# Six value buffers, five probability buffers, attention loads moved ahead, and first products that wait for half of a weight unit

## The chip, the cores and the metric

The kernel runs on one core of a Trainium2 chip. The metric is the device time of one execution in microseconds (us). Five engines work side by side, each through its own instructions in their order: PE (TensorE, matrix products), DVE (VectorE), ACT (ScalarE), POOL (GpSimd) and SP (SyncE), which here only issues transfers. They wait for each other through semaphores.

## What is computed

```python
attn = softmax_masked(q @ k.T / 8) @ v            # q, k, v: (2, 8, 576, 64)
# heads 0..3: keys of the last 32 positions; heads 4..7: keys at the same position modulo 32
x = attn.transpose(0, 2, 1, 3).reshape(1152, 512)
h = np.maximum(x @ w_in, 0.0)                     # w_in (512, 2048)
x = h * h @ w_out                                 # w_out (2048, 512)
p = domain_probs / domain_probs.sum(-1)           # (1152, 4)
out = sum(p[:, e:e+1] * (np.maximum(x @ w1[e], 0.0) @ w2[e]) for e in range(4))
```

The weights of the first pair (w_in, w_out) come as 64-bit numbers; the kernel makes two 32-bit parts of each itself.

## The kernel before

Attention is cut into 16 groups: `Strided` (heads 4 to 7, 8 units of 54 or 36 queries) and `Local` (heads 0 to 3, 128 or 64 queries). One group (`attend`, L461) is: three loads (k, q, v), scores on PE (L363 to L367 or L430 to L438), maximum on DVE (L485), exponentials on ACT (L490, or L495 on DVE and L496 on ACT), sums and reciprocals on DVE (L497 to L499), normalizing on POOL (L500), transposes on PE (L372 or L442), a copy on ACT (L480), products with the values on PE (L384 or L452), and the result into x in two parts, on ACT (L509) and DVE (L513). Six groups are `startup`, seven `second`, three `third`.

The first pair of products runs over x in three blocks of 384 tokens (x_75, x_76, x_77 in the order's names) and over weight units in w buffers (w_80 to w_89). A unit is loaded and converted in two halves (L562): a 512 KB load (L568), ACT (L575), three DVE steps (L580, L584, L589), ACT (L595) and POOL (L599). A product of 128x384 stands as three matmuls, L617, L618 and L619, which the text calls a round. Four rounds into a bank bh make one step x @ w_in (L639); relu and square follow on ACT and DVE (L650, L654, L657, L660), and give h; four rounds into banks by are its h @ w_out (L681). The first eight steps use block x_75 alone, and need eight units, w_80 to w_87. Afterwards blocks 1 and 2 use the same units again. The experts (L834 to L836, and L617 to L619 again) follow, and are not touched by the change.

The order of everything is made when the program is built: `Plan.run` takes tasks with estimated lengths, rank, needs and buffer rings, and starts on each engine the ready task of lowest rank. The instructions are then written in the order of these starts. A change of a ring, a rank or an estimate thus reorders all engines. While PE has nothing before its first products, the plan puts in matmuls on a zero tile (`warm`, L961), called fillers below. Rings that matter here: q and k with 4 buffers, v with 4 (`NQ`), p (probabilities) with 3 (`NP`), and 2 banks ba for attention, beside banks by in the first six groups.

Of the kernel before, what the change touches and what calls it, by code (L numbers as in the profile page):

```python
# [16 lines left out]
P = 128  # L17
B, H, S, D = 2, 8, 576, 64
# [3 lines left out]
TB = 384  # L22
NB = NT // TB
KD = DM // P
CH = 256
# [136 lines left out]
def tile_attention_mlp_experts(ctx: ExitStack, tc: tile.TileContext, a, out):  # L162
# [20 lines left out]
    def many(pool, name, n, shape, dtype=F32):  # L183
        return [pool.tile(shape, dtype, name=f"{name}{i}") for i in range(n)]
# [7 lines left out]
    CONV0 = 7431  # L192
    CONV = 9000
    FETCH = 2019
    WITH2 = 1082
    PE_SLICE = 863
    BASE = 3959
# [10 lines left out]
    NMID = 2  # L208
    NHID = 4
    NST = 5  # L210
    NP = 3
    NQ = 4
    NPT = 2
    NW = 10
    NS = 2
# [20 lines left out]
    plan.ring("bank_y", many(banks, "by", 4, [P, 512]))  # L236
    plan.ring("q", many(at, "q", NQ, [P, U * N3]))
    plan.ring("k", many(at, "k", NQ, [P, U * N3]))
    plan.ring("v", many(at, "v", NQ, [P, 512]))
    probs = many(at, "p", NP, [P, 512])  # L240
    plan.ring("p", probs)
    plan.ring("pt", many(at, "pt", NPT, [P, 512]))
# [9 lines left out]
    def mm_r(n):  # L252
        return int(n / 2.4) + 3
# [4 lines left out]
    def act(n):  # L258
        return n + 40
# [5 lines left out]
        return int(n * 2.05) + 190  # L265

    def dma(nbytes):
        return int(nbytes / 357) + 60


    n1, n2 = FF // P, F2 // P
# [5 lines left out]
    def due(n):  # L277

        return START + STEP * n + WITH * min(n, half) + WITH2 * min(max(n - half, 0), half)

# [177 lines left out]
    x_ready = {}  # L458
    attention_done = []

    def attend(g, rank, rings):  # L461
        env = {}
        n = g.units * g.cols
        loads = []
        for what, nbytes in zip("kqv", g.bytes):
            loads.append(plan.add({"dma": dma(nbytes)}, lambda e, w=what: g.load(env, w), rank=rank - 5000, take=[(env, what, [what])]))

        def view(x, pitch=g.pitch):
            return x[:, : g.units * pitch].rearrange("p (u c) -> p u c", u=g.units)[:, :, : g.cols]
# [50 lines left out]

    startup = [Strided(0, j) for j in range(3)] + [Local(0, j) for j in range(3)]
    for k, g in enumerate(startup):
        attend(g, BASE + EACH * k, ["bank_a", "bank_y"])
    second = [Local(0, 3), Local(0, 4)] + [Strided(1, j) for j in range(3)] + [Local(1, 0), Local(1, 1)]
    for k, g in enumerate(second):
        attend(g, START - AHEAD + k * (due(half) - START - END2) // len(second), ["bank_a"])
    third = [Local(1, j) for j in (2, 3, 4)]
    for k, g in enumerate(third):
        attend(g, due(half) - AHEAD + k * (due(2 * half) - due(half) - END3) // len(third), ["bank_a"])

    def open_late(e):
        attn.close()
# [23 lines left out]
    for u in sorted(when, key=lambda x: when[x]):  # L556
        kind, e_, c = u
        w_env[u] = {}
        wide_ = kind in ("wi", "wo")
        soon = wide_ and first[u] <= LAG  # L560
        rank = when[u] - (CONV0 if soon else CONV)
        for j in range(2):  # L562
            env = {}
            cs = slice(j * 2 * CH, (j + 1) * 2 * CH)

            def load(e, env=env, kind=kind, e_=e_, k=2 * c + j, wide_=wide_):
                if wide_:
                    nc.sync.dma_start(out=env["raw"], in_=a[kind][k].bitcast(U32))  # L568
                else:
                    nc.sync.dma_start(out=f32(env["raw"][:, : 2 * CH]), in_=a[kind][e_, k])  # L570

            def small(e, env=env):
                top = f32(env["raw"].rearrange("p (f t) -> p f t", t=2)[:, :, 1])
                if e == "act":
                    nc.scalar.activation(out=env["mid"], in_=top, func=AF.Copy, scale=EXP_SHIFT)  # L575
                else:
                    nc.vector.tensor_scalar(out=env["mid"], in0=top, scalar1=EXP_SHIFT, scalar2=None, op0=ALU.mult)

            def shift(e, env=env):
                nc.vector.tensor_scalar(out=env["val"].bitcast(U32), in0=env["mid"].bitcast(U32), scalar1=3, scalar2=0x7FFFFFF8, op0=ALU.logical_shift_left, op1=ALU.bitwise_and)  # L580

            def sign(e, env=env):
                v = env["val"].bitcast(U32)
                nc.vector.scalar_tensor_tensor(out=v, in0=env["mid"].bitcast(U32), scalar=0x80000000, in1=v, op0=ALU.bitwise_and, op1=ALU.bitwise_or)  # L584

            def low(e, env=env):
                v = env["val"].bitcast(U32)
                bits = env["raw"].rearrange("p (f t) -> p f t", t=2)[:, :, 0]
                nc.vector.scalar_tensor_tensor(out=v, in0=bits, scalar=29, in1=v, op0=ALU.logical_shift_right, op1=ALU.bitwise_or)  # L589

            def value(env=env, wide_=wide_):
                return env["val"] if wide_ else f32(env["raw"][:, : 2 * CH])

            def hi(e, u=u, cs=cs, value=value):
                nc.scalar.activation(out=weights(u)[:, 0, cs], in_=value(), func=AF.Copy)  # L595

            def lo(e, u=u, cs=cs, value=value):
                w = weights(u)
                eng[e].tensor_tensor(out=w[:, 1, cs], in0=value(), in1=f32(w[:, 0, cs]), op=ALU.subtract)  # L599

            t = plan.add({"dma": dma(P * 4 * CH * 4 if wide_ else P * 2 * CH * 4)}, load, after=[chain["dma"]], rank=rank - FETCH, take=[(env, "raw", ["raw"])])
            chain["dma"] = t
            n = 2 * CH
            if wide_:
                t = plan.add({"act": act(n)}, small, after=[t], rank=rank, take=[(env, "mid", ["mid"])])
                t = plan.add({"dve": dve(n // 2)}, shift, after=[t], rank=rank + 500, take=[(env, "val", ["val"])])
                t = plan.add({"dve": dve(n)}, sign, after=[t], rank=rank + 700, free=[(env, "mid")])
                t = plan.add({"dve": dve(n)}, low, after=[t], rank=rank + 1200, free=[(env, "raw")])
            t = plan.add({"act": act(n)}, hi, after=[t, chain["w"]], rank=rank + 2000, take=[(w_env[u], "w", ["w"])] if j == 0 else [], quiet=not wide_)
            chain["w"] = t  # L610
            lo_engines = {"pool": pool(n)} if wide_ else {"dve": dve(n)}
            t = plan.add(lo_engines, lo, after=[t], rank=rank + R_LO, free=[(env, "val") if wide_ else (env, "raw")], quiet=not wide_)
            w_ready.setdefault(u, []).append(t)
# [19 lines left out]
    for n in range(moe1 + LAG):  # L633
        if n < moe1:
# [3 lines left out]
            for pos, kk in enumerate((2, 3, 0, 1)):  # L638
                def product(e, env=env, u=u, b=b, i=i, kk=kk, pos=pos):  # L639
                    w = w_in(u)  # L640
                    cs = slice((i % 2) * P, (i % 2 + 1) * P)
                    mm3(env["H"][:, :TB], w[:, 0, kk, cs], w[:, 1, kk, cs], xt[b][:, 0, kk], xt[b][:, 1, kk], pos == 0, pos == 3)

                freed = [(w_env[u], "w")] if pos == 3 and last_use[u] == n else []
                previous = plan.add({"pe": 3 * mm_r(TB)}, product, after=[previous if pos else None, *x_ready[b, (0, 1) if kk < 2 else (2, 3)], *w_ready[u]], rank=due(n) + pos * PE_SLICE, take=[(env, "H", ["bank_h"])] if pos == 0 else [], free=freed, adds=[("bank_y", [spare])] if n == 0 and pos == 0 else ())
            t = previous
            rank = due(n) - URGENT

# [402 lines left out]
```

## Time and profile before

| | |
|---|---|
| median of 3 runs | 647.59 us (647.18 to 648.01) |
| profiled execution | 647.54 us, of it span of the trace 645.8 us |
| PE busy | 631.5 us, 98% of the span |
| DVE busy | 360.8 us, 56% |
| ACT, POOL busy | 235.6 us, 105.9 us |

The span is measured from the first instruction to the last. "Busy" of PE counts modelled ends of overlapping matmuls, so that a share near 100% says that PE has no idle gap, and not that it is at its peak. A gap of an engine is shown in brackets with what ended it.

### The profile page before, as it was taken

What the parts mean: (1) busy time and instruction counts of PE and PEld (TensorE: products, weight loads), DVE (VectorE), ACT (ScalarE), POOL (GpSimd) and SP (SyncE); (2) the same over time, 40 slices, a digit from 0 to 9 for tenths busy, and PEclk for the clock granted to TensorE, in tenths of its full rate; (3) what the DMA queues carried; (4) which work ended last, traced back from release to release, by engine and by line L of the source; (5) the groups of instructions that cost most, each with busy time, mean ns of one, the idle gap of its engine ahead of it and who ended that gap; (6) DMA issues with size and microseconds to landing.
All of it is one profiled execution on the core that took longest, in us unless ns stands there. A gap on an engine that the chain in (4) does not pass through costs nothing.

```text
span 645.8 us, 9891 instructions
## 1 busy us (share of the span) xinstructions
PE 631.5 (98%) x3868; PEld 580.2 (90%) x3868; DVE 360.8 (56%) x664; ACT 235.6 (36%) x527; POOL 105.9 (16%) x119
## 2 busy tenths in 40 slices
PE   7998999999999999999999999999999999999997
PEld 4777889999999999999999999999999999999997
DVE  4898886288623264945557415557324557643512
ACT  2956675354423244522333312333212333321110
POOL 2435341033100000030112000113001012400000
PEclk9998999999999999999999999999999999999999
DMA  8976434034300023231133301123301222100201
GB/s 276 265 228 179 150 127 131 0 100 145 98 1 1 1 65 98 72 91 38 38 94 136 89 1 50 63 90 110 81 1 50 81 82 97 33 2 0 98 2 49
DMA packets 28990, 53.51 MB, mean 83 GB/s; under 512 B 4432, under 2 KB 10000, under 8 KB 28944
## 3 DMA queue, kind: packets, MB, share of 16 engines
q1 hardware_dynamic: 28944, 52.89, 26.7%
q8 instruction: 30, 0.49, 0.3%
q14 instruction: 16, 0.13, 0.1%
HBM read 50.52 MB, written 2.36 MB: 82 GB/s over the span
## 4 chain that ended last, share of the span: by engine, by line
PE 88%; DVE 5%; ACT 2%; DMA 2%; issue 1%; POOL 1%; SPq 1%; DVEq 0%; ACTq 0%; POOLq 0%
PE bh L617 14%; PE bh L618 14%; PE bh L619 14%; PE by L835 8%; PE by L836 8%; PE by L834 8%; PE by L617 5%; PE by L619 4%; PE by L618 4%; PE ba L836 2%; PE ba L835 2%; PE ba L834 2%; DVE val L580 1%; DVE val L589 1%; DVE val L584 1%
## 5 line engine op out<-in xcount | busy, mean ns | idle before, releaser
L617 PE MATMUL bh<-x,w 128*128 128x384 f32 x416 | 141.8, 341 | 1.7 <-DVE h L660 1.7
L619 PE MATMUL bh<-x,w 128*128 128x384 f32 x416 | 139.8, 336 | 0.0
L618 PE MATMUL bh<-x,w 128*128 128x384 f32 x416 | 139.7, 336 | 0.0
L872 DVE TENSOR_TENSOR c<-bh,c 128x384 f32<-128x384 f32 x80 | 43.1, 556 | 85.9 <-ACT c L885 58.4
L836 PE MATMUL by<-w,h 128*128 128x512 f32 (+1 forms) x232 | 89.0, 384 | 0.0
L835 PE MATMUL by<-w,h 128*128 128x512 f32 (+1 forms) x232 | 89.0, 384 | 0.0
L834 PE MATMUL by<-w,h 128*128 128x512 f32 (+1 forms) x232 | 88.5, 382 | 0.0
L617 PEld LDWEIGHTS bh<-x,w 128*128 128x128 f32 x416 | 78.5, 189 | 4.7 <-DVE h L660 3.2
L618 PEld LDWEIGHTS bh<-x,w 128*128 128x128 f32 x416 | 78.5, 189 | 1.0
L619 PEld LDWEIGHTS bh<-x,w 128*128 128x128 f32 x416 | 78.4, 188 | 0.0
L779 POOL TENSOR_TENSOR sf<-raw 128x256 f32<-128x256 f32 x16 | 12.1, 755 | 347.1 <-DMA raw<-in_w_dram 283.8
L617 PE MATMUL by<-h,w 128*128 128x384 f32 x192 | 65.5, 341 | 0.3 <-ACT h L657 0.3
L618 PE MATMUL by<-h,w 128*128 128x384 f32 x192 | 64.5, 336 | 0.6 <-DVE h L660 0.6
L619 PE MATMUL by<-h,w 128*128 128x384 f32 x192 | 64.6, 336 | 0.0
L599 POOL TENSOR_TENSOR w<-val,w 128x512 fp32r<-128x512 f32 x32 | 43.3, 1361 | 76.4 <-ACT w L595 73.9
L654 DVE SCALAR_TENSOR_TENSOR bh<-bh,r 128x384 f32<-128x384 f32 x48 | 27.0, 562 | 51.0 <-ACT r L650 51.0
L929 DVE SCALAR_TENSOR_TENSOR h<-bh,h 128x384 fp32r<-128x384 f32 x32 | 17.8, 557 | 64.0 <-ACT h L926 64.0
L904 ACT ACTIVATE h<-c 128x384 fp32r<-128x384 f32 x64 | 31.8, 518 | 54.6 <-DVE c L872 34.5
L836 PEld LDWEIGHTS by<-w,h 128*128 128x128 f32 x232 | 43.6, 188 | 8.5
L834 PEld LDWEIGHTS by<-w,h 128*128 128x128 f32 x232 | 43.6, 188 | 8.0
L835 PEld LDWEIGHTS by<-w,h 128*128 128x128 f32 x232 | 43.6, 188 | 8.1
L599 DVE TENSOR_TENSOR w<-raw,w 128x512 fp32r<-128x512 f32 x64 | 43.1, 696 | 9.3 <-ACT w L595 9.3
(122 smaller groups left out, 1039.2 us busy)
## 6 DMA issues: line engine op xcount, KB each, us to landing
raw<-in_w_dram SPq DMA_DIRECT2D x64, 256.0 KB, 2.7
raw<-in_wi_dram SPq DMA_DIRECT2D x16, 512.0 KB, 3.7
raw<-in_wo_dram SPq DMA_DIRECT2D x16, 512.0 KB, 3.6
raw<-in_w_dram SPq DMA_DIRECT2D x16, 512.0 KB, 3.6
out_dram<-acc SPq DMA_DIRECT2D x8, 256.0 KB, 2.1
v<-in_vs_dram SPq DMA_DIRECT2D x6, 256.0 KB, 4.4
v<-in_vl_dram SPq DMA_DIRECT2D x8, 192.0 KB, 3.8
k<-in_kl_dram SPq DMA_DIRECT2D x8, 160.0 KB, 4.5
```

What stands on the lines that cost most here:

```text
L599: eng[e].tensor_tensor(out=w[:, 1, cs], in0=value(), in1=f32(w[:, 0, cs]), op=ALU.subtract)
L617: nc.tensor.matmul(dst, lhsT=wh, rhs=xh, start=start, stop=False)
L618: nc.tensor.matmul(dst, lhsT=wh, rhs=xl, start=False, stop=False)
L619: nc.tensor.matmul(dst, lhsT=wl, rhs=xh, start=False, stop=stop)
L654: nc.vector.scalar_tensor_tensor(out=h, in0=h, scalar=0.0, in1=env["r"], op0=ALU.max, op1=ALU.mult)
L779: nc.gpsimd.tensor_tensor(out=got(env["sf"])[:, 0], in0=part(env, 1, 0), in1=part(env, 1, 1), op=ALU.add)
L834: nc.tensor.matmul(o, lhsT=h[:, 0, ts], rhs=w[:, 0], start=start, stop=False)
L835: nc.tensor.matmul(o, lhsT=h[:, 0, ts], rhs=w[:, 1], start=False, stop=False)
L836: nc.tensor.matmul(o, lhsT=h[:, 1, ts], rhs=w[:, 0], start=False, stop=stop)
L872: return lambda e: nc.vector.tensor_tensor(out=got(c[key]), in0=c[bank][:, :TB], in1=got(c[other]), op=ALU.add)
L904: nc.scalar.activation(out=env["hid"][:, 0], in_=got(c[key]), func=AF.Relu)
L929: nc.vector.scalar_tensor_tensor(out=env["hid"][:, 1], in0=env["H"][:, :TB], scalar=0.0, in1=f32(env["hid"][:, 0]), op0=ALU.max, op1=ALU.s ...
```

## The change

The value ring gets six buffers of its own (`NV`), the probability ring five. The loads of the six startup groups get a rank 9000 ahead of their scores, the later ones 3500, where all had 5000. The estimated length of a load grows (310 bytes per ns instead of 357). The halves of a w_in unit are taken in the order 1, 0, and a product waits for the half that it reads, where it waited for both; x rows 2 and 3, which it takes first, are in half 1. FIRST is 0 and changes nothing.

```diff
-    NP = 3
+    NP = 5
     NQ = 4
+    NV = 6
+    LEAD0, LEAD = 9000, 3500
...
-    plan.ring("v", many(at, "v", NQ, [P, 512]))
+    plan.ring("v", many(at, "v", NV, [P, 512]))
...
-        return int(nbytes / 357) + 60
+        return int(nbytes / 310) + 60
...
-            loads.append(plan.add({"dma": dma(nbytes)}, lambda e, w=what: g.load(env, w), rank=rank - 5000, take=[(env, what, [what])]))
+            loads.append(plan.add({"dma": dma(nbytes)}, lambda e, w=what: g.load(env, w), rank=rank - lead, take=[(env, what, [what])]))
...
-        for j in range(2):
+        for j in (1, 0) if kind == "wi" else (0, 1):
...
-            t = plan.add({"act": act(n)}, hi, after=[t, chain["w"]], rank=rank + 2000, take=[(w_env[u], "w", ["w"])] if j == 0 else [], quiet=not wide_)
+            t = plan.add({"act": act(n)}, hi, after=[t, chain["w"]], rank=rank + 2000, take=[(w_env[u], "w", ["w"])] if u not in w_ready else [], quiet=not wide_)
...
-  after=[previous if pos else None, *x_ready[b, (0, 1) if kk < 2 else (2, 3)], *w_ready[u]]
+  after=[previous if pos else None, *x_ready[b, (0, 1) if kk < 2 else (2, 3)], w_ready[u][kk < 2]]
```

In the changed kernel all lines behind the edits stand three lower (L620 is the old L617). Names below end in the buffer's number.

**SP, loads of the first groups.** k, q, v are attention loads, raw is half of a weight unit. Before:

```order
L424 DMA v_122<-in_vl_dram 96x512
L568 DMA raw_90<-in_wi_dram 128x1024
L420 DMA k_115<-in_kl_dram 128x2x160
L422 DMA q_111<-in_ql_dram 128x256
L420 DMA k_116<-in_kl_dram 128x2x160
L422 DMA q_112<-in_ql_dram 128x256
L420 DMA k_117<-in_kl_dram 128x2x160
L568 DMA raw_91<-in_wi_dram 128x1024
```

After:

```order
L427 DMA v_122<-in_vl_dram 96x512
L423 DMA k_115<-in_kl_dram 128x2x160
L425 DMA q_111<-in_ql_dram 128x256
L427 DMA v_123<-in_vl_dram 96x512
L423 DMA k_116<-in_kl_dram 128x2x160
L425 DMA q_112<-in_ql_dram 128x256
L427 DMA v_124<-in_vl_dram 96x512
L571 DMA raw_90<-in_wi_dram 128x1024
```

Six loads of groups 5 and 6, their values among them, now stand ahead of the first weights.

**PE, around the first product of the first pair (L617, later L620).** Before:

```order
L384 MATMUL ba_106<-pt_126,v_121 64x36 x16
L442 MATMUL ba_105<-ident,p_124 96x128 x4
L452 MATMUL by_108<-pt_127,v_122 64x64 x8
L617 MATMUL bh_103<-x_75,w_80 128x384
L618 MATMUL bh_103<-x_75,w_80 128x384
L619 MATMUL bh_103<-x_75,w_80 128x384
```

After:

```order
L445 MATMUL by_108<-ident,p_125 96x128 x4
L436 LDWEIGHTS cb
L436 MATMUL ba_105<-cb 128x192
L441 MATMUL ba_105<-k_118,q_114 64x96 x4
L366 LDWEIGHTS cb
L366 MATMUL ba_106<-cb 128x432
L370 MATMUL ba_106<-k_115,q_111 54x54 x16
L455 MATMUL by_107<-pt_131,v_122 64x64 x8
L455 MATMUL ba_105<-pt_130,v_123 64x64 x8
L620 MATMUL bh_103<-x_75,w_80 128x384
```

The first product now stands behind the scores of two more groups (nine in all; before, seven) and behind a fifth set of value products.

**PE, where blocks of attention meet the products with w_83 (h_99 is the third h).** Before:

```order
L438 MATMUL ba_106<-k_118,q_114 64x96 x8
L617 MATMUL by_109<-h_99,w_83 128x384
L618 MATMUL by_109<-h_99,w_83 128x384
L619 MATMUL by_109<-h_99,w_83 128x384
L617 MATMUL by_108<-h_99,w_83 128x384
```

After:

```order
L441 MATMUL ba_106<-k_118,q_114 64x96 x8
L375 MATMUL ba_105<-ident,p_125 128x128 x4
L436 LDWEIGHTS cb
L436 MATMUL ba_105<-cb 128x192
L441 MATMUL ba_105<-k_115,q_111 64x96 x4
L387 MATMUL ba_106<-pt_130,v_123 64x36 x16
L620 MATMUL by_110<-h_99,w_83 128x384
```

Transposes, scores and value products of three groups, which were spread between products, now follow each other in the two banks ba.

**DVE, at the same place.** Before:

```order
L589 SCALAR_TENSOR_TENSOR val_95<-raw_90,val_95 128x512
L584 SCALAR_TENSOR_TENSOR val_96<-mid_94,val_96 128x512
L499 RECIPROCAL st_132<-st_132 128x8
L589 SCALAR_TENSOR_TENSOR val_96<-raw_91,val_96 128x512
L495 TENSOR_TENSOR p_124<-ba_105,st_128 128x8x36
```

After:

```order
L592 SCALAR_TENSOR_TENSOR val_95<-raw_90,val_95 128x512
L501 TENSOR_SCALAR st_132<-st_132 128x8
L502 RECIPROCAL st_132<-st_132 128x8
L516 TENSOR_TENSOR x_76<-ba_105,x_76 128x2x6x12
L583 TENSOR_SCALAR val_96<-mid_94 128x512
L657 SCALAR_TENSOR_TENSOR bh_103<-bh_103,r_101 128x384
L587 SCALAR_TENSOR_TENSOR val_96<-mid_94,val_96 128x512
L516 TENSOR_TENSOR x_77<-ba_105,x_77 128x24x12
L657 SCALAR_TENSOR_TENSOR bh_104<-bh_104,r_102 128x384
L663 TENSOR_TENSOR h_99<-bh_103,h_99 128x384
L592 SCALAR_TENSOR_TENSOR val_96<-raw_91,val_96 128x512
L663 TENSOR_TENSOR h_100<-bh_104,h_100 128x384
```

The eighth half of a weight unit (val_96 from raw_91), which followed the seventh closely, now comes behind results of attention and behind two squares.

## Rows read from the trace of the kernel before

**Rows 1.** By stretch: us, busy PE, PEld, DVE, ACT, POOL, granted clock, DMA share, GB/s.

```profile
5.00:28.00 23.00, 18.74 (x326) 13.42 (x323) 15.77 (x47) 12.93 (x52) 7.77 (x8) 1.00 1.01 298
28.00:45.00 17.00, 15.75 (x215) 13.34 (x212) 16.68 (x34) 11.15 (x28) 7.41 (x7) 1.00 0.79 243
45.00:61.00 16.00, 13.38 (x143) 11.46 (x143) 14.61 (x31) 8.94 (x20) 6.81 (x6) 0.98 0.66 194
61.00:71.00 10.00, 10.00 (x81) 9.24 (x79) 8.26 (x18) 7.50 (x24) 4.87 (x5) 0.86 0.45 150
...
110.00:646.00 536.00, 531.87 (x2806) 496.85 (x2804) 272.38 (x475) 168.75 (x337) 63.94 (x76) 1.00 0.19 60
```

**Rows 2.** PE's waits from 5 to 110 us: total us, times, longest.

```profile
PE ba L438 <- DMA q<-in_ql_dram: 2.4, 2, 1.4
PE ba L433 <- DVE x L513: 1.9, 1, 1.9
PE bh L617 <- DVE h L660: 1.1, 2, 0.9
...
PE ba L372 <- POOL p L500: 0.7, 1, 0.7
...
PE ba L363 <- DVE x L513: 0.2, 1, 0.2
```

**Rows 3.** Timeline of ACT and PE, first weights: start, length, what, idle before.

```profile
14.17 0.66 ACT L575 ACTIVATE mid<-raw 128x512 f32<-128x512 f32 x1 [3.66 <-DMA raw<-in_wi_dram]
...
26.61 0.44 PE L617 MATMUL bh<-x,w 128*128 128x384 f32 x1
```

**Rows 4.** Loads: how often, KB each, median us from issue to landing.

```profile
v<-in_vl_dram SPq DMA_DIRECT2D x8, 192.0 KB, 3.8
k<-in_kl_dram SPq DMA_DIRECT2D x8, 160.0 KB, 4.5
q<-in_ql_dram SPq DMA_DIRECT2D x8, 128.0 KB, 4.5
```

**Rows 5.** Timeline of PE: scores and value products of strided groups.

```profile
36.84 1.01 PE L367 MATMUL ba<-k,q 64*54 64x54 f32 x32
...
47.10 1.14 PE L384 MATMUL ba<-pt,v 54*64 54x54 f32 x32
```

**Rows 6.** Timeline of DVE and POOL: conversion steps beside POOL and alone.

```profile
33.16 2.55 POOL L599 TENSOR_TENSOR w<-val,w 128x512 fp32r<-128x512 f32 x2 [1.28 <-ACT w L595]
...
34.49 1.50 DVE L580 TENSOR_SCALAR val<-mid 128x512 uint32<-128x512 uint32 x1
...
37.03 0.41 DVE L580 TENSOR_SCALAR val<-mid 128x512 uint32<-128x512 uint32 x1
...
56.08 0.67 DVE L584 SCALAR_TENSOR_TENSOR val<-mid,val 128x512 uint32<-128x512 uint32 x1
56.19 1.71 POOL L599 TENSOR_TENSOR w<-val,w 128x512 fp32r<-128x512 f32 x1 [4.08 <-ACT w L595]
...
56.90 1.55 DVE L589 SCALAR_TENSOR_TENSOR val<-raw,val 128x512 uint32<-128x512 uint32 x1
```

**Rows 7.** Groups from 0 to 110 us: count, busy us, mean ns, idle before.

```profile
L580 DVE TENSOR_SCALAR val<-mid 128x512 uint32<-128x512 uint32 x22 | 15.4, 699 | 4.9 <-ACT mid L575 4.3 <-POOL w L599 0.3
```

**Rows 8.** The chain that ended last: exponentials of one local group.

```profile
82.48 1.40 ACT p L490 x8
```

**Rows 9.** Timeline of PE: the longest wait, half clock, and full clock.

```profile
58.87 0.24 PE L433 MATMUL ba<-cb 128*128 128x192 bf16 x1 [1.93 <-DVE x L513]
...
61.14 0.53 PE L618 MATMUL by<-h,w 128*128 128x384 f32 x1
61.46 0.53 PE L619 MATMUL by<-h,w 128*128 128x384 f32 x1
...
83.34 0.33 PE L619 MATMUL bh<-x,w 128*128 128x384 f32 x1
83.51 0.33 PE L617 MATMUL bh<-x,w 128*128 128x384 f32 x1
```

More of the change, by code (lines that the diff above doesn't have):

```diff
@@ L194, in tile_attention_mlp_experts @@
     FETCH = 2019
+    FIRST = 0
     WITH2 = 1082
@@ L459, in tile_attention_mlp_experts, with attend @@
     attention_done = []
-    def attend(g, rank, rings):
+    def attend(g, rank, rings, lead):
         env = {}
@@ L522, in tile_attention_mlp_experts @@
     for k, g in enumerate(startup):
-        attend(g, BASE + EACH * k, ["bank_a", "bank_y"])
+        attend(g, BASE + EACH * k, ["bank_a", "bank_y"], LEAD0)
     second = [Local(0, 3), Local(0, 4)] + [Strided(1, j) for j in range(3)] + [Local(1, 0), Local(1, 1)]
     for k, g in enumerate(second):
-        attend(g, START - AHEAD + k * (due(half) - START - END2) // len(second), ["bank_a"])
+        attend(g, START - AHEAD + k * (due(half) - START - END2) // len(second), ["bank_a"], LEAD)
     third = [Local(1, j) for j in (2, 3, 4)]
     for k, g in enumerate(third):
-        attend(g, due(half) - AHEAD + k * (due(2 * half) - due(half) - END3) // len(third), ["bank_a"])
+        attend(g, due(half) - AHEAD + k * (due(2 * half) - due(half) - END3) // len(third), ["bank_a"], LEAD)
     def open_late(e):
@@ L599, in lo @@
                 eng[e].tensor_tensor(out=w[:, 1, cs], in0=value(), in1=f32(w[:, 0, cs]), op=ALU.subtract)
-            t = plan.add({"dma": dma(P * 4 * CH * 4 if wide_ else P * 2 * CH * 4)}, load, after=[chain["dma"]], rank=rank - FETCH, take=[(env, "raw", ["raw"])])
+            t = plan.add({"dma": dma(P * 4 * CH * 4 if wide_ else P * 2 * CH * 4)}, load, after=[chain["dma"]], rank=rank - FETCH - (FIRST if first.get(u) == 0 else 0), take=[(env, "raw", ["raw"])])
             chain["dma"] = t
@@ L644, in tile_attention_mlp_experts @@
                 freed = [(w_env[u], "w")] if pos == 3 and last_use[u] == n else []
-                previous = plan.add({"pe": 3 * mm_r(TB)}, product, after=[previous if pos else None, *x_ready[b, (0, 1) if kk < 2 else (2, 3)], *w_ready[u]], rank=due(n) + pos * PE_SLICE, take=[(env, "H", ["bank_h"])] if pos == 0 else [], free=freed, adds=[("bank_y", [spare])] if n == 0 and pos == 0 else ())
+                previous = plan.add({"pe": 3 * mm_r(TB)}, product, after=[previous if pos else None, *x_ready[b, (0, 1) if kk < 2 else (2, 3)], w_ready[u][kk < 2]], rank=due(n) + pos * PE_SLICE, take=[(env, "H", ["bank_h"])] if pos == 0 else [], free=freed, adds=[("bank_y", [spare])] if n == 0 and pos == 0 else ())
             t = previous
```

## The prediction

> **What bounds the kernel now.** I read first the busy time by stretch [rows 1]. The reader is to see that from 110 us on PE is busy 531.9 of 536.0 us, and what is missing there is the end of the program. So the time after 110 us is the sum of the products, which the change leaves alone, and the change can only gain or lose what PE loses before. Next the same table for the beginning. From 28 to 45 us DVE is busy 16.7 of 17.0 us, from 45 to 61 us 14.6 of 16.0. There PE is fed by DVE: no round starts before DVE has converted its weights or has finished its h. From 61 us on PE has no gap for 10 us, since block 1 of x is there by then and each converted unit is used twice. Before 28 us the transfers are the limit: DMA share 1.01, 298 GB/s. Then PE's waits [rows 2]: thirteen rows, 9.3 us in all when added up, the longest single one 1.9 us for DVE's x. Last the clock: it is 0.98 and 0.86 in the stretches 45 to 61 and 61 to 71 [rows 1], which is 0.02 x 16 + 0.14 x 10 = 1.7 us lost; matmuls there start 0.32 us apart, at 1.2 GHz, where they start 0.17 us apart at 2.4 [rows 9], and the fall came after the 1.93 us wait. So 9.3 + 1.7 = 11.0 us, and the few fillers that stand in further gaps before the first product, are all that any order could give back.
>
> I count in PE's work: how much further PE is in the new order at the same time. Since PE is never short of work later, that lead at 110 us is the gain. The profiled execution took 647.54 us, the median is 647.59; I add to the first.
>
> **The first weights, 5 to 28 us.** The new order puts six loads ahead of the first half of weights: 2 x (192 + 160 + 128) KB [rows 4] = 0.98 MB, at 298 GB/s 3.3 us. The half landed at 14.1 us [rows 3] and will land near 17.4. Behind it on ACT stand its own copy, the exponentials of a group (1.40 us, rows 8) and the copy of the second half, which lands some 4 us later (the next six loads with the second half are 1.2 MB). I lay the new order on these lengths and find the first half ready on POOL near 25.0 us, and the first product at 28.0, where it was at 26.6 [rows 3]. Waiting for one half instead of two saves one conversion here (DVE 0.41 + 0.67 + 0.67 us [rows 6], then ACT and POOL), and hides most of the 3.3 us. In exchange PE has done one more set of scores (1.0 us) and one more of value products with its transposes (at most the 1.1 us of a strided group) [rows 5], against 1 or 2 rounds of 0.52 us less. The lead at 28 us is 1.0 to 1.6; I take 1.5, since the fifth probability buffer lets ACT and POOL go through the first groups without a stop. The two added buffers cost two more clears on POOL at the very start, where POOL is idle until its first normalizing.
>
> **28 to 45 us.** By the order, DVE has as many conversions behind it when it makes the first h, and more of the attention; it starts that h without the 1.5 us step that met POOL [rows 6]. Walked through, the two first h are done at 37 and 38 us, some 2.4 us earlier, and PE, which waits 1.6 us for the first of them, has at 45 us three rounds and one set of transposes and values more behind it: lead 2.5.
>
> **45 to 61 us: what the change adds.** Here the new order sets attention and h ahead of the eighth half of weights on DVE: a sum, a subtraction, four pieces of x, two squares and a part of h, nine steps that at 0.4 to 0.7 us each [rows 6] are 4 to 6 us. PE stands behind it: the rounds with w_83 need that half, and ahead of them three pieces of attention follow each other in two banks, each waiting for the one before it. Waits, in order: transposes for POOL's normalizing, 0.6 (0.7 at such a place now, rows 2); value products for ACT's copy behind another group's exponentials, 1.5; transposes for a bank that DVE empties, 1.0; scores for the copy out of the same bank, 1.0; and value products for a bank in which the exponentials of the next group have yet to run: 0.6 of DVE, 1.4 of ACT [rows 8], and 1.3 us more if DVE's small step runs into a POOL weight step of 1.28 us (2.55 for two, rows 6): 2.0 to 3.3, middle 2.65. Together 6.75 us. Now this stretch has 0.7 + 1.9 = 2.6 [rows 2]. The lead falls by 4.15, to -1.65.
>
> The step of 1.3 us hangs on a meeting: L580 takes 0.41 us alone and 1.50 beside POOL, L589 1.55 [rows 6], and over 22 steps L580 averages 0.70 [rows 7]. POOL's step at 56.19 took 1.71 us, and began inside DVE's L584, which ended at 56.75. The Trainium skill, "SBUF — State Buffer", section "SBUF: two separate sides", says that the two engines hold a shared port pair by an exclusive lock, for whole instructions, and that whichever starts first makes the other wait. The trace agrees both ways round: 56.75 plus 1.28 is 58.03, and POOL ended at 57.90. By that rule a shift of 0.1 us in the order of starts decides over 1.3 us, which is why I take the middle here.
>
> **The clock.** A wait over 1.9 us stands in the new stretch too, so I let the clock fall as before, but half of the low stretch under waits: 0.85 of the 1.7 us is kept. Lead -0.8.
>
> **61 to 110 us.** Block 1 of x is complete on DVE some 2 us earlier, so PE has rounds to put into the gaps while DVE converts the last units. I take the two waits for h, 1.1 us [rows 2], as gone. Lead +0.3.
>
> **Edits with one answer.** FIRST is 0: nothing. The longer estimate for loads moves a few loads and ACT and DVE steps behind 110 us, under a PE that does not wait: nothing. If that cover fails, a late half unit costs one conversion, some 4 us once. SP's queue is passed by value loads that had to wait for a buffer; no wait in rows 2 is for values, so this pays only through the weights queued behind them.
>
> Sum: 1.5 + 1.0 - 4.15 + 0.85 + 1.1 = 0.3 us gained, **647.2 us**.
>
> **Rivals.** (1) Faster: DVE and POOL miss each other in 28 to 61 us. Then the last wait is 2.0, and the earlier ones shrink too, since each contains a step of DVE that was pushed: I found 4.1 us instead of 7.4 with no meeting at all. The lead at 61 us is 2.5 - 1.5 = 1.0, and with 0.85 and 1.1 the gain is 3.0; if no wait is long enough for the clock to fall, 3.8: 643.7 to 644.6. For it: the new order has fewer stops before 45 us. Against it: POOL has as many steps as before. (2) Slower: the waits of 45 to 61 us come in full (7.4), and the clock falls twice for it, since they surround a stretch with hardly a product: 1.5 + 1.0 - 4.8 - 1.7 + 1.1 with nothing kept of the first fall = -2.9, so 650.4; with one fall and none of it under waits, 648.7. It decides from a fifth wait above 3 us. (3) The buffers change nothing: the lead of the beginning is spent by 45 us because DVE's work is the same, and PE waits as now: 647.5. What speaks for it: DVE is busy 98% from 28 to 45 us whatever the order.
>
> **How the numbers follow.** A measurement here tells 0.2%, 1.3 us, from no change. The forecast, 646.3 to 648.8, has 0.33, the third case 0.07, both within 0.2%; faster has 0.35, slower 0.25. The likeliest single mechanism is the forecast's, its time 647.2. For the range I go to 643.2 below (the faster case and a little of the beginning's 1.6 us more) and to 650.4 above, the slower case; that leaves some 0.15 out. Faster 0.35, same 0.40, slower 0.25.
>
> **What would show it.** In the profile after: the first ACT step on raw near 17.5 us; the first L620 near 28; first h on DVE near 37, the second near 38; PE waits of 5 to 7 us together between 45 and 61, the longest on value products (L387) after exponentials; a low clock within 65 us; no wait for h after 71. A first product after 29.5 us would break the first step; PE waits under 4 us in 45 to 61 would mean the faster case; a low clock in two stretches the slower one. PE waits after 110 us would break the sum at its root.

## The result and the profile after

| | before | after |
|---|---|---|
| median | 647.77 us (647.18 to 648.01, 4 runs) | 652.51 us (651.99 to 653.97, 4 runs) |
| ratio | | 1.0068, 95% interval 1.0044 to 1.0092 |
| profiled execution, span | 647.54, 645.8 us | 652.63, 650.9 us |

The change makes the kernel 0.7% slower. The forecast was 647.2 us with a range from 643.2 to 650.4; the time lies above the range.

The busy times by stretch, in the columns of [rows 1]; the last two rows are the stretches in which the clock was low:

```profile
5.00:28.00 23.00, 18.38 (x327) 13.51 (x326) 16.15 (x45) 13.14 (x50) 7.34 (x8) 0.98 0.95 299
28.00:45.00 17.00, 16.76 (x237) 14.09 (x234) 14.98 (x32) 11.24 (x28) 7.58 (x7) 0.92 0.71 203
45.00:61.00 16.00, 10.25 (x104) 8.77 (x104) 14.94 (x34) 8.77 (x25) 5.39 (x5) 0.91 0.64 199
61.00:71.00 10.00, 10.00 (x77) 9.02 (x78) 7.22 (x15) 4.82 (x19) 4.85 (x5) 0.64 0.38 113
...
110.00:651.00 541.00, 536.41 (x2833) 501.63 (x2831) 275.60 (x485) 171.60 (x342) 65.34 (x77) 1.00 0.20 62
...
27.30:30.60 3.30, 3.30 (x64) 3.11 (x62) 2.51 (x8) 2.51 (x9) 2.23 (x3) 0.50 0.17 63
...
58.00:68.20 10.20, 7.32 (x59) 6.39 (x60) 8.70 (x17) 4.68 (x20) 5.30 (x5) 0.50 0.61 197
```

From 45 to 61 us PE is busy 10.25 us where it was 13.38 [rows 1], and from 61 to 71 us it is busy all the time, but at a clock of 0.64. The records put the low clock (1.2 GHz) at 27.25 to 30.67 and at 57.97 to 68.21 us; before there was one such stretch, 60.48 to 63.89. What is missing after 110 us is 4.6 us of 541, where it was 4.1 of 536 [rows 1]; 1.2 us of it are waits for h, before 0.6.

PE's waits over the whole run, as in [rows 2]:

```profile
PE ba L387 <- ACT p L493: 3.2, 1, 3.2
PE bh L620 <- DVE h L663: 2.3, 4, 0.8
PE ba L436 <- ACT p L493: 1.6, 1, 1.6
...
PE ba L387 <- ACT pt L483: 1.0, 1, 1.0
PE by L445 <- POOL p L503: 0.9, 1, 0.9
PE ba L375 <- DVE x L516: 0.8, 1, 0.8
PE ba L436 <- ACT pt L483: 0.8, 1, 0.8
```

The four rows with 3.2, 1.0, 0.8 and 0.8 us are the attention chain in 45 to 61 us. PE's timeline there (start, length, what, idle before and its releaser):

```profile
53.88 0.88 PE L441 MATMUL ba<-k,q 64*64 64x96 f32 x16
55.55 0.63 PE L375 MATMUL ba<-ident,p 128*128 128x128 f32 x4 [0.79 <-DVE x L516]
56.94 0.24 PE L436 MATMUL ba<-cb 128*128 128x192 bf16 x1 [0.76 <-ACT pt L483]
57.11 0.55 PE L441 MATMUL ba<-k,q 64*64 64x96 f32 x8
60.88 1.92 PE L387 MATMUL ba<-pt,v 36*64 36x36 f32 x32 [3.22 <-ACT p L493]
62.73 0.69 PE L620 MATMUL by<-h,w 128*128 128x384 f32 x1
63.22 0.52 PE L621 MATMUL by<-h,w 128*128 128x384 f32 x1
63.54 0.52 PE L622 MATMUL by<-h,w 128*128 128x384 f32 x1
```

Between 53.9 and 60.9 us PE does 2.3 us of work, all of it pieces of attention, and not one round. The low clock begins 0.3 us into the long wait. When the wait ends, PE has work without a gap, but until 68.21 the matmuls of a round start 0.32 us apart, where they start 0.17 us apart at the full clock [rows 9].

To see where the time went I count work: each instruction of PE at the median length that it has over the traces, fillers left out, added up to a given time in both traces. The difference is the lead of a kernel over the one before, in us of PE's work. It is good to some 0.3 us, since matmuls overlap and their overlap can be counted in more than one way:

| at us | 24 | 28 | 45 | 56 | 61 | 71 | 110 | 200 |
|---|---|---|---|---|---|---|---|---|
| after | 1.3 | 0.4 | -0.2 | -0.9 | -2.8 | -4.5 | -4.7 | -5.0 |
| forecast | | 1.5 | 2.5 | | -1.65 | -0.8 | 0.3 | 0.3 |

The 5.0 at 200 us are the 5.1 by which the span grew. Clock and waits overlap in this row, so it says when the time was lost and not yet to what. The experiments part the two. Their kernels carry added lines, so that an instruction stands a few lines lower there (L620 as L631, L387 as L389, L516 as L527). A run is said to be at full clock when its mean granted clock is 0.999 or 1.0. All ratios are to the kernel before, run on the same chip.

### The profile page after: what moved, and what is told of

It is laid out like the page before. It is cut to its first block, busy times and chain, and to the rows that moved or that the text cites. A ratio compares the mean times of both kernels' runs of the same rounds, so it can differ in the third digit from the quotient of the medians.

```text
span 650.9 us, 9891 instructions
## 1 busy us (share of the span) xinstructions
PE 633.6 (97%) x3863; PEld 583.0 (90%) x3863; DVE 360.5 (55%) x664; ACT 236.7 (36%) x527; POOL 106.9 (16%) x121
## 4 chain that ended last, share of the span: by engine, by line
PE 88%; DVE 5%; DMA 3%; issue 2%; ACT 1%; SPq 1%; POOL 0%; DVEq 0%; ACTq 0%; POOLq 0%
PE bh L620 14%; PE bh L622 14%; PE bh L621 14%; PE by L838 8%; PE by L839 8%; PE by L837 8%; PE by L620 4%; PE by L622 4%; PE by L621 4%; PE ba L839 2%; PE ba L838 2%; PE ba L837 2%; DVE val L592 1%; DVE val L583 1%; DMA raw<-in_wi_dram 1%
## 5 line engine op out<-in xcount | busy, mean ns | idle before, releaser
L620 PE MATMUL bh<-x,w 128*128 128x384 f32 x416 | 141.6, 340 | 2.4 <-DVE h L663 2.3
L620 PEld LDWEIGHTS bh<-x,w 128*128 128x128 f32 x416 | 78.3, 188 | 5.6 <-DVE h L663 3.9
L620 PE MATMUL by<-h,w 128*128 128x384 f32 x192 | 65.8, 343 | 0.0
L907 ACT ACTIVATE h<-c 128x384 fp32r<-128x384 f32 x64 | 31.8, 519 | 54.5 <-DVE c L875 34.4
L663 DVE TENSOR_TENSOR h<-bh,h 128x384 fp32r<-128x384 f32 x48 | 26.6, 555 | 39.3 <-ACT h L660 39.1
```

Source lines behind the costliest of these rows:

```text
L620: nc.tensor.matmul(dst, lhsT=wh, rhs=xh, start=start, stop=False)
L663: nc.vector.tensor_tensor(out=env["hid"][:, 1], in0=env["H"][:, :TB], in1=f32(env["hid"][:, 0]), op=ALU.subtract)
L907: nc.scalar.activation(out=env["hid"][:, 0], in_=got(c[key]), func=AF.Relu)
```

## Experiments: the clock or the waits

**The clock kept up.** Matmuls of the identity were put ahead of the waiting instruction, into columns that nobody reads (cut down to what matters; each stands as two in the trace):

```diff
+    for _ in range(n):
+        nc.tensor.matmul(spare[:, TB:512], lhsT=ident, rhs=ident, start=False, stop=False)
...
-  lambda e: g.values(env)
+  lambda e: (g.fill("v"), g.values(env))     # Strided(1, 2): n = 14
```

> The changed kernel with 14 matmuls of the identity put on PE ahead of the value products (L387) that waited 3.22 us at 57.66 to 60.88 us; they go into columns 384 to 511 of a bank that the program never reads there, and lie within the wait. Theory A (the time was lost by the clock: 1.2 GHz from 57.97 to 68.21 us, and PE had work there from 60.88 on, 7.3 us, so some 3.65 us): the fall ends much sooner or does not come, 648.9 us if it goes, 650.6 if a fall as long as the first (3.41 us) is left. Theory B (the waits themselves and the order of DVE's work cost the time, the clock is a bystander): 652.5, since the wait still ends when the exponentials are done.

Measured: 1.0029 (1.0006 to 1.0051). PE's timeline and the same stretch by engines:

```profile
56.30 3.39 PE L469 MATMUL by<-ident 128*128 128x128 f32 x28
59.63 1.13 PE L387 MATMUL ba<-pt,v 36*64 36x36 f32 x32
60.68 0.45 PE L631 MATMUL by<-h,w 128*128 128x384 f32 x1
60.97 0.34 PE L632 MATMUL by<-h,w 128*128 128x384 f32 x1
```

```profile
54.00:58.00 4.00, 2.98 (x28) 2.55 (x29) 4.00 (x9) 2.05 (x4) 1.26 (x1) 1.00 0.59 177
58.00:68.20 10.20, 10.20 (x102) 9.37 (x100) 7.82 (x19) 6.53 (x27) 4.91 (x6) 1.00 0.47 167
```

The wait is as long as before (3.3 us from the end of the scores to the value products), but the same value products take 1.13 instead of 1.92 us, the clock is 1.00 where it was 0.50, and 0.0039 of the 0.0068 come back. That is the profiled execution. Only three of the ten runs were at full clock, with a median of 649.5 us; the seven others had a mean clock of 0.990 to 0.995 and took 650.0 to 653.1 us. So fillers in this one wait do not keep the clock up every time.

> The changed kernel with matmuls put into six waits of PE: 4 and 6 of the zero tile in the waits of 0.95 and 1.57 us at 22.8 to 26.0 us, 4, 3, 3 and 14 of the identity in those of 0.97, 0.79, 0.76 and 3.22 us at 49.3 to 60.9. Theory A: neither fall of the clock (27.25 to 30.67, 57.97 to 68.21 us) comes; 3.65 us come back from the second and 0.8 from the first, where PE's work fell 0.75 us behind: 648.1 us, near the kernel before. Theory B: 652.5 us, a clock that stays up and a first h that is no earlier.

Measured: 1.0020 (1.0006 to 1.0035). All ten runs were at full clock and lay within 649.2 and 651.1 us. So some 3 us of the loss went with the low clock (1.0068 to 1.0020, with intervals that do not meet), less than theory A's 648.1 us asked for. With the clock out of play the changed order still costs about 2.3 us: the ten have a median of 649.65, and the 30 runs of the kernel before at full clock, of 115 in all comparisons, one of 647.4.

**The wait shortened.** The maximum, its scaling and the exponentials on which the value products wait were set ahead, the first two behind the scores on DVE, the third behind the copy of another group on ACT, and nothing else moved in the order (the scaling's edit is left out here):

```diff
+        if (type(g), g.b, g.j) == (Local, 1, 0):
+            t.like = (scores, 0.1)
...
+            if (type(g), g.b, g.j) == (Local, 1, 0):
+                t.like = (copied["Strided", 1, 2], 0.1)
```

> The changed kernel with the maximum, its scaling and the exponentials of one group (Local(1, 0), whose scores end at 54.8 us) set ahead on DVE and ACT: the maximum behind its scores instead of behind two h and a weight step, the exponentials ahead of two weight steps of ACT. All else stands as it was. The value products that waited 3.22 us can start 2.6 us earlier, near 58.3. If the clock alone cost the time, the second fall (57.97 to 68.21 us) shrinks to at most 3.4 us or goes and this comes to the ratio that filling that wait gave, 1.003 to before. If the wait costs beside the clock, up to 2.6 us more come back: 0.999 to 1.000. If what follows waits for DVE's weights anyhow, the 2.6 us turn up again as waits before 75 us, and the ratio is 1.003 or more.

Measured: 1.0068 (1.0046 to 1.0091), the changed kernel's ratio. PE's timeline, then the stretches:

```profile
55.54 0.63 PE L377 MATMUL ba<-ident,p 128*128 128x128 f32 x4 [1.91 <-DVE x L527]
56.93 0.24 PE L438 MATMUL ba<-cb 128*128 128x192 bf16 x1 [0.76 <-ACT pt L486]
57.10 0.55 PE L443 MATMUL ba<-k,q 64*64 64x96 f32 x8
58.22 1.93 PE L389 MATMUL ba<-pt,v 36*64 36x36 f32 x32 [0.57 <-ACT p L499]
```

```profile
54.00:58.20 4.20, 1.35 (x13) 0.84 (x13) 3.35 (x8) 2.30 (x11) 0.00 (x0) 1.00 0.58 175
58.30:68.40 10.10, 9.34 (x66) 8.28 (x67) 7.43 (x16) 4.90 (x18) 5.23 (x5) 0.50 0.41 129
```

The value products start at 58.22, 2.7 us earlier, as expected. Of that, 1.3 us are the beginning, which had no early fall here: in fill_long, where it had none either, the exponentials ended at 59.57 us, in the changed kernel at 60.83. And the wait for x ahead of the transposes grew from 0.79 to 1.91 us, so that the waits from 45 to 61 us are 4.2 us together, where they were 5.7. Yet the clock falls at 58.20 all the same, stays low until 68.44, and the 2.7 us are gone by 71 us. So the wait of 3.22 us was not needed for the fall. What the two executions share is a stretch ahead of it in which PE had little work: 1.35 of 4.20 us here, 2.10 of 4.00 us in the changed kernel. But such a stretch does not always bring a fall. The changed kernel and no_npnv, one of the kernels of the next section:

```profile
54.00:58.00 4.00, 2.10 (x29) 1.41 (x29) 4.00 (x9) 2.83 (x6) 0.00 (x0) 1.00 0.55 162
54.00:58.00 4.00, 1.49 (x20) 1.11 (x20) 4.00 (x9) 2.99 (x7) 1.22 (x1) 1.00 0.45 146
```

In no_npnv PE did still less there, with one wait of 2.51 us, and the clock stayed up. In the same way the wait of 1.93 us of the kernel before [rows 2] had a fall 1.6 us behind it, and its like of 1.91 us in nosign_before (further below), with much the same rounds ahead of it and behind it, had none. So neither the length of a wait nor the work around it foretells the fall in one execution, and what sets it off stays open.

> The kernel of the run before last (maximum and exponentials of Local(1, 0) set ahead, so that the 3.22 us wait is 0.57) with matmuls of the identity in the waits that are left there (4, 8, 3, 2 and 3 of them at 49.2, 55.5, 56.9, 58.2 and 62.2 us). The fourth corner: the wait shorter and the clock kept up. Both alone gave 1.0068 (wait shorter, clock fell) and 1.0029 (wait whole, clock up), the changed kernel 1.0068. If the clock is what costs and the wait only its trigger, this is 1.002 to 1.003, as with the wait whole. If the wait costs too once the clock is up, 0.999 to 1.000. If the fillers did it by something else than the clock, 1.0068.

Measured: 1.0050 (1.0033 to 1.0067), above the 1.003 of the case that it came nearest to; five of eight runs were at full clock, with a median of 650.9, but the profiled one had a low stretch at 62.15 to 65.56. The four corners, as lead won or lost from 45 to 71 us and as ratio:

| | clock low from 58 to 68 us | clock kept up (in the last one, low for 3.4 us) |
|---|---|---|
| wait of 3.2 us | -4.3, 1.0068 | -1.5, 1.0029 |
| wait of 0.6 us | -4.6, 1.0068 | -2.4, 1.0050 |

Keeping the clock up is worth 2.2 to 2.8 us; the shorter wait is worth nothing in either column. Runs at full clock say the same: 650.9 us with the shorter wait, 649.5 (fill_long) and 649.65 (fill_all) with the whole one, and 647.4 to 647.5 for the kernel before on either chip. Their fillers are not the same, so the difference of 1.3 us is not the wait's alone. What the shorter wait frees turns up in other waits (the 1.91 us ahead of it, 0.76 us at 62.15).

**The same in the kernel before.**

> The kernel before with 8 matmuls of the identity in its 1.93 us wait ahead of scores at 56.94 to 58.87 us. Theory A: its only fall (60.48 to 63.89 us) goes, and the 1.7 us lost there come back: 646.1 us. Theory B: 647.8, as before.

> The kernel before with matmuls in the same three waits (3 of the zero tile at 23 us, 3 and 8 of the identity at 49.6 and 58.9 us). Its runs with a granted clock of 1.0 took 646.1 to 647.2 us, those with less up to 650.7. If the clock is the cause of that spread, nearly all runs are 646.5 to 647.5 and the ratio 0.998; if not, 1.000 with the same spread.

Measured: 1.0000 (0.9980 to 1.0021) and 1.0003 (0.9984 to 1.0021). In both profiled executions the low stretch is gone, and in the first PE is 0.9 us ahead at 68 us; at 71 us it is 0.2 behind, after a wait of 1.2 us for ACT's copy. The 1.7 us of [rows 1] were not there to be won: the fall of before lies in front of a wait that ends when ACT and DVE are done. The fillers did not bring all runs to a full clock, 4 and 5 of 10 had one, so the two ratios do not price the fall by themselves. The runs of the kernel before do: the 46 of the 115 with a mean clock of 0.997, that of the profiled execution with its one fall, have a median of 647.9 us, the 30 at full clock one of 647.4. One fall goes with some 0.6 us there, not 1.7.

## Experiments: which part of the change

One part undone, or one part alone (in short form; left the changed kernel or the kernel before, right the run):

```diff
no_half    -  w_ready[u][kk < 2]            +  *w_ready[u], halves in order 0, 1
no_lead0   -  LEAD0, LEAD = 9000, 3500      +  LEAD0, LEAD = 5000, 3500
no_npnv    -  NP = 5, NV = 6                +  NP = 3, NV = 4
no_dma     -  int(nbytes / 310) + 60        +  int(nbytes / 357) + 60
b_half     before, with the half wait and the order 1, 0 alone
b_lead     before, with LEAD0, LEAD = 9000, 3500 alone
```

> The changed kernel, but a product waits for both halves of its unit and the halves come in order 0, 1 as before; buffers, leads and the load estimate stay. If the half wait is to blame (it lets PE take rounds one at a time, so that few are left to put into the waits at 49 to 61 us), the rounds with the third unit come together and the waits there stay under 3 us: 648 us. If not, the first weights land as late (18.9 us on ACT), the first product is at 30 us or later, and the time is 652 or more.

> The changed kernel with the loads of the first six groups back at 5000 ahead, the later ones at 3500; all else as changed. If the late first weights are the cause (ACT's first step on raw at 18.9 us where it was 14.2, the second raw at 23.1), the first step is back at 14 to 15 us, the first product comes by 27 us, and the time is 647.8 or less. If the cause is the order at 49 to 61 us, which depends on rounds being at hand there, the order there is another one and the result depends on its waits: with less than 3 us of them 648, else 650 or more.

> The kernel before with one part of the change: halves of a unit in the order 1, 0, and a product waits for its half. Buffers, leads and the estimate as before. If the half wait is of use by itself, the first product is 1 to 2 us earlier (it saves one conversion of 0.41 + 0.67 + 0.67 us on DVE) and the time 646.5; if it only hands rounds out early, which then lack in later waits, 648 to 649.

> The kernel before with one part of the change: the first six groups' loads 9000 ahead, the later ones 3500. Value buffers are four, so that values 5 and 6 can't pass the weights. If the leads cause the loss: first raw on ACT 3 to 4 us later than 14.2, the first product after 28 us, and 650 us or more. If not: 647.8.

> The changed kernel with three probability and four value buffers, as before; leads, estimate and half wait as changed. The leads alone put the first h at 46 us and cost 1.0114. If the added buffers are what lets the early loads go without that loss, this is as slow: 1.008 to 1.012, first h after 42 us. If the buffers do nothing, it is as the changed kernel, 1.0068, first h at 37 to 39 us.

> The changed kernel with the estimated length of a load as before (357 bytes per ns). If the estimate changes nothing before 110 us but a few loads, first h at 37 to 39 us, and the time is the changed kernel's, 1.005 to 1.008, with the long wait near 58 us and the low clock behind it. If its order is the other one that the estimate gives, in which the rounds of one unit stand alternately with the next, the waits in 45 to 61 us are shorter than 3 us and it is 1.000 to 1.003.

Measured, with the first h step on DVE and the low stretches of the profiled execution up to 100 us:

| | ratio (95%) | first h, us | lead at 45, 71, 200 us | low clock at, us |
|---|---|---|---|---|
| changed | 1.0068 (1.0044 to 1.0092) | 38.6 | -0.2, -4.5, -5.0 | 27.3 to 30.7, 58.0 to 68.2 |
| no_half | 1.0047 (1.0024 to 1.0069) | 37.7 | 0.4, -1.1, -2.9 | 59.4 to 62.8 |
| no_lead0 | 1.0085 (1.0054 to 1.0115) | 45.0 | -5.3, -3.6, -5.7 | 28.4 to 31.8, 38.6 to 42.0 |
| no_npnv | 1.0027 (1.0013 to 1.0041) | 41.5 | -3.3, -2.0, -2.6 | 35.4 to 38.8 |
| no_dma | 1.0111 (1.0088 to 1.0134) | 44.9 | -5.3, -5.0, -7.8 | 11.2 to 18.0, 28.3 to 35.1, 55.6 to 59.0 |
| b_half | 1.0045 (1.0022 to 1.0068) | 38.7 | 0.2, 1.9, -0.9 | 83.0 to 86.4 |
| b_lead | 1.0114 (1.0090 to 1.0137) | 46.2 | -4.9, -2.7, -5.7 | 29.4 to 36.2, 90.8 to 94.2 |

The parts do not add up, and with any one of them undone a loss is left. The leads alone cost 1.1%, more than the whole change, and their first h comes 7 us late (46.2 us, before 38.9); within the whole change, taking the first lead back makes it no better. The half wait alone is 1.9 us ahead at 71 us, and loses that in two waits at 81 and 152 us and a fall at 83. The longer estimate, which the forecast put at nothing, is worth 0.4% within the change, and the buffers, put at nothing as well, cost 0.4%: without them the first h comes later, but the stretch from 45 to 71 us is no loss. A part of those 0.4% goes with the clock, since the runs without the buffers had a mean clock of 0.992 to 0.997, those of the changed kernel 0.990 to 0.994. Of the six expectations only that for b_lead named its time and first product (31.5 us), and there ACT's first step on raw came at 13.6 us, no later than before; the others came out between or beyond their cases. Each edit makes the planner lay another order, and as far as these runs tell, the time is that order's, not the edit's.

## Experiments: what sets the pace beside the clock

The same order of PE, ACT and POOL, with less work for DVE:

```diff
 def sign(e, env=env, u=u):
+    if first.get(u, 99) < 5 and u[2] < 2:
+        return                               # eight steps of 0.68 us
```

> The changed kernel with matmuls in the 3.22 us wait (the run that came to 1.0029), less one DVE step (L587, the sign of the weights, 0.68 us) for each of the eight halves of the first four units of weights; so this kernel leaves out the sign of those weights and is run for its time alone. The order of PE, ACT and POOL is the same. 5.4 us of DVE's work before 60 us go. If what is left of the loss is DVE's work (PE stands behind conversions and h), PE is 2 to 4 us further at 71 us and the ratio falls to 0.997 to 1.000. If it is the chain of attention pieces in two banks, which passes through ACT and POOL, at most 0.5 us come back: 1.002 to 1.003.

> The kernel before less the same eight DVE steps (the sign of the first four units' weights is left out, the time alone counts). DVE is busy 16.7 of 17 us from 28 to 45 there. If DVE sets the pace, PE is 2 to 4 us further at 71 us: 643.5 to 645.5 us, 0.994 to 0.997. If not, 647.5.

Measured: 0.9958 (0.9941 to 0.9974) for the changed kernel with its clock kept up, all ten runs at full clock; 0.9993 (0.9974 to 1.0011) for the kernel before, none of its ten at full clock. The stretch from 45 to 61 us of the first:

```profile
45.00:61.00 16.00, 15.16 (x176) 13.24 (x175) 13.33 (x31) 10.20 (x30) 6.91 (x7) 1.00 0.61 201
```

of the second, where the longest wait is still 1.9 us long and still for x:

```profile
PE ba L433 <- DVE x L513: 1.9, 1, 1.9
```

In the changed order 5.4 us less of DVE's work make 4.6 us by the ratios (1.0029 to 0.9958), but not all of it is DVE's: fill_long was at full clock in three of ten runs only. At full clock the medians are 649.5 and 646.1 us, and those of the kernel before on the two chips 647.4 and 647.65; that leaves 3.6 us, and 0.9976 as the ratio, inside what was expected for DVE. So DVE's work sets most of the pace there. It could be more, since the fillers kept PE until 57.09 us, 1.2 us longer than the exponentials took. In the kernel before the same work is worth nothing that can be measured (at a mean clock of 0.997, 647.6 us without it and 648.1 with it). That DVE is busy 16.7 of 17 us there [rows 1] did not mean that PE's pace was DVE's.

> The changed kernel with matmuls in the 3.22 us wait (1.0029) and without one small DVE step of each attention group (L501, which adds 1e-9 to a sum of exponentials that is at least 1): 16 steps, 3.3 us of DVE in that run, some 2.5 us of them before 60 us. If DVE's work sets the pace there (8 steps of 0.68 us less, 5.4 us, gave 0.0071), these 2.5 to 3.3 us give 0.003 to 0.004: a ratio of 0.999 to 1.000. If only the steps of the weights' chain count, 1.003.

```diff
-  lambda e: nc.vector.tensor_scalar(out=stat(1), in0=stat(1), scalar1=1e-9, scalar2=None, op0=ALU.add)
+  lambda e: None
```

Measured: 1.0000 (0.9980 to 1.0021), as expected. By all runs this interval meets that of fill_long. At full clock the two part: 646.9 to 648.0 us in six runs here, 649.0 to 649.5 in three of fill_long. So steps outside the weights' chain count as well, as far as these nine runs go.

Why a small step of DVE can be dear is seen on another one, L495, beside POOL. DVE and POOL of the changed kernel, ahead of the long wait's end:

```profile
58.11 1.23 DVE L495 TENSOR_SCALAR st<-st 128x4 f32<-128x4 f32 x1
...
60.12 0.15 DVE L495 TENSOR_SCALAR st<-st 128x2 f32<-128x2 f32 x1
```

```profile
58.03 1.28 POOL L602 TENSOR_TENSOR w<-val,w 128x512 fp32r<-128x512 f32 x1 [4.34 <-ACT w L598]
```

Four numbers per partition took 1.23 us instead of some 0.16: the step ended 0.03 us after POOL's, and the exponentials stood behind it. The Trainium skill, "SBUF — State Buffer", section "SBUF: two separate sides", says that the port pair which DVE and POOL share is held for a whole instruction and the other engine is fully blocked; this trace agrees, with 1.28 us of POOL and 1.23 of DVE.

**Two steps of h set ahead.** In the half-wait kernel, the last DVE step of h 6 and of h 21 was put ahead of the one weight step before it; half_best adds fillers, half_lean drops the step above too.

```diff
+ if n in (6, 21):
+     env["ready"].like = (t, 0.1)
```

> The kernel before with the half wait alone (it was 2 us ahead of the kernel before at 75 us and lost them again in two waits for h, 1.6 us at 81.5 and 2.0 at 152.1, and in a low clock from 83 to 86.4), and the last DVE step of h number 6 and of h number 21 set ahead of the one weight step that stood before each (1.73 us and 1.67 us, both beside a POOL step). If these two steps are the cause, the waits fall to 0.5 us each, the clock does not fall at 83, and 2 us are kept: 645.5 us against 647.5, a ratio of 0.997. If weights are then late instead, a wait of like size stands elsewhere and the ratio stays 1.000 to 1.0045.

> The same as half_h, with matmuls in three waits of PE (3 of the zero tile at 23 us, 3 of the identity each at 49.6 and 56.9 us). If the spread of its runs is the clock's, the runs lie close together and the ratio is 0.995 to 0.997; if not, as half_h.

> The kernel before with the half wait, the two h steps set ahead and matmuls in three waits (0.999), less the same small DVE step of each group (4.4 us of DVE in that run). If its waits for h (1.0, 1.2 and 1.3 us from 85 us on) and for x stem from DVE's work, 2 to 3 us come back: 0.995, faster than both kernels. If it is bound by the chain from engine to engine, as the kernel before seems to be (eight steps less gave it nothing), 0.998 to 1.000.

Measured: 1.0005 (0.9987 to 1.0022), 0.9990 (0.9971 to 1.0009) and 0.9984 (0.9967 to 1.0002). Against 1.0045 for the half wait alone, the two steps give back 0.004: the clock no longer falls at 83 us, and eight of ten runs are at full clock, where none was. But the waits did not shrink together, they moved: waits of 1.0 to 1.3 us stand at 84.3, 105.4 and 155.6 us instead of 1.7 and 2.0 at 81.5 and 152.1. So again the gain goes with the clock. The last one, within what was expected for a chain from engine to engine, is at best 0.3% faster than the kernel before, and its interval just includes no change; none of the three is faster than the kernel before beyond the measurement.

## Why the forecast was wrong, step by step

**5 to 28 us, lead 1.5: wrong in the profiled execution, right beside it.** The first ACT step on raw came at 18.94 us (17.5 forecast), the first half unit began on POOL at 24.37 and was ready at 26.1 (25.0), the first L620 came at 30.63, beyond the 29.5 that was to break this step. ACT and PE there:

```profile
21.24 0.63 ACT L512 ACTIVATE x<-by 128x288 fp32r<-128x288 f32 x2
23.11 0.67 ACT L578 ACTIVATE mid<-raw 128x512 f32<-128x512 f32 x1 [1.25 <-DMA raw<-in_wi_dram]
```

```profile
25.99 0.24 PE L436 MATMUL ba<-cb 128*128 128x192 bf16 x1 [1.57 <-ACT p L493]
...
30.63 0.44 PE L620 MATMUL bh<-x,w 128*128 128x384 f32 x1
```

ACT stood at the copy of the second half until 23.11, with the exponentials of a group behind it; PE waited 1.57 us for them, and the clock fell. The step named those exponentials as standing behind the copy, but gave ACT's standing still no price. In the three kernels that are the same up to 49 us (fill_long, early, early_fill) that copy came at 21.4 to 21.7, no fall came, the first product came at 28.6 to 28.8, and the lead at 28 us was 1.3 to 1.4.

**28 to 45 us, +1.0: wrong.** The first two h were done at 39.1 and 40.1 us; in fill_long at 37.8 and 38.8, near the forecast (37, 38; before 39.4 and 40.5). But the lead did not grow with them: 1.36 to 1.21 in fill_long, 0.4 to -0.2 in the profiled execution, part of it under the low clock. The step reads a wait of 1.6 us for the first h; the trace of the kernel before has 0.27 us for ACT's part and 0.56 for DVE's, 0.8 together, so there was half of that to win, and in fill_long, where PE came there earlier too, the wait is 0.9. The rounds that were to be three more by 45 us were not there: by the records some 12 were done in the changed kernel and 15 in fill_long, before nearly 16.

**45 to 61 us, -4.15: right in kind, a little too dear.** The four waits of the chain came in the order foretold, 0.97, 0.79, 0.76 and 3.22 us, 5.7 together where 6.75 stood (the one for POOL, 0.6, did not come). The last had bounds of 2.0 and 3.3, with POOL's step as the difference, and the meeting took place. The lead fell by 2.6, or 3.1 with the clock up.

**The clock, +0.85: the step that failed most.** It assumed one fall as long as that of before, half of it under waits. From 61 to 71 us 3.6 us were lost at a clock of 0.64, where 1.4 were lost before [rows 1]: the lead fell by another 1.7, 2.5 away from the forecast. The forecast tied the fall to the length of a single wait. But it came 0.31 us into the long wait, it came as well where that wait was 0.57 us, and behind 2.51 us in no_npnv it did not come: the length of a wait does not tell it, and no run here shows what does. The term's size was off too: in the kernel before a fall goes with some 0.6 us and not 1.7, so there was little to be kept of it. With the clock up in every run (fill_all) 2.3 us of loss stay where 0.3 us of gain were forecast, so the clock is a little over half of the miss; the rest lies in the two gains, +1.0 and +1.1, that did not come.

**61 to 110 us, +1.1: wrong.** The waits for h stayed: 1.1 us by 110 and 2.3 in the whole run (1.1 and 1.7 before). The low clock is not what kept them: in fill_long, at full clock throughout, PE waits 2.1 us for h by 110 us.

**The edits with one answer: wrong.** The estimate and the buffers were to cost nothing; undone, they move the time by 0.4% each, in opposite directions, the buffers in part through the clock.

**The rivals.** The slower one (waits in full, the clock falls twice) came nearest, with the wait above 3 us that it named. It is not quite what happened: the waits were 5.7 us and not 7.4, and the first of the two falls came at 27.25 us, ahead of the stretch that it blamed, and stands in some executions only. Its 650.4 was 2 us short: it took each fall to be as long as the one before, and kept 2.5 us of lead from the beginning. Of the forecast's 0.3 us the terms miss 1.1, 1.6, -1.5, 2.5, 1.3 and 0.3 (the last after 110 us), together 5.3.

Open remains why the beginning differs so much between executions of one order (the second raw half landed at 21.4 to 23.1 us); with that, whether a given execution has the early fall cannot be foretold from one trace.

## What to carry to other kernels

Do not price the clock by the longest wait alone: ask also how much matmul work stands around the waits, and where little does, carry a case in which the next stretch runs at half clock. It is a chance and not a rule, as no_npnv shows. Filler matmuls in such a place are cheap to try and part the clock's share from the wait's, but only when runs of the same mean clock are compared. Where a planner lays the order, an edit to a buffer count or an estimate is not free, here it moved the time by 0.4%; undo each part by itself before giving the loss to one.

## What was not expected of the hardware

The clock stayed at 1.2 GHz for 10.24 us where the kernel before had it there for 3.41, and 7.3 us of that PE had no gap at all. In the kernel before a run's time goes with its mean granted clock: of 115 runs, 30 with 0.999 or 1.0 had a median of 647.4 us, 46 with 0.997 one of 647.9, 12 with 0.992 or less one of 650.7. Whether the clock makes that difference, or falls because something else made the run late, these numbers do not tell; and two kernels should be compared at the same mean clock, since the changed kernel's four runs had 0.990 to 0.994.
